# Gated linear attention into a mixture of experts: attention pieces moved together on TensorE, the state update in 64-column halves

## The chip, the cores and the metric

The kernel runs on 1 core of one Trainium2 chip. The metric is the device time of the whole launch in microseconds (us), lower is better. The span that the profile gives runs from the first to the last instruction of the program in one profiled execution.

## The reference

Two stages follow each other. For each of B = 4 batches and H = 8 heads a recurrence over S = 768 steps with head size D = 48, and then four experts on the 3072 rows that it gives:

```python
for t in range(S):
    state = alpha[:, :, t, :, None] * state + np.einsum('bhd,bhe->bhde', k[:, :, t], v[:, :, t])
    y[:, :, t] = np.einsum('bhd,bhde->bhe', q[:, :, t], state)
...
x = y.transpose(0, 2, 1, 3).reshape(B * S, H * D)        # 3072 x 384
p = domain_probs / (domain_probs.sum(-1, keepdims=True) + 1e-09)
for e in range(E):                                       # 4 experts, F = 1024
    h = np.maximum(x @ w1[e], 0.0)
    out += p[:, e:e + 1] * (h @ w2[e])
```

Everything is float32.

## The kernel before

**Units.** The sequence is cut into 6 blocks of 128 steps. One block of one batch, with its 8 heads, is a *unit*; there are 24. `attention(u)` is a Python generator that issues a unit's work in 17 *pieces*, one for each `next`; they are counted from 0 here:

- pieces 0 to 2 transpose alpha, k and q on TensorE (`turned`, L262 to L266) and copy or multiply them out of PSUM; each also issues the next unit's load on SyncE's queue;
- pieces 3 to 6 scale q and k level by level (`copy_q` on ScalarE, `next_q` on VectorE, `next_k` on both);
- piece 7 makes the *first scores*, levels 0 to 3, on TensorE (`products`, L333: 32 matmuls, each with 64 stationary columns, into PSUM tiles `sc`), and `take` (L343, VectorE) picks two of them out; piece 8 takes the other two; pieces 7 to 10 go on with `next_q`, `next_k`, `copy_q` for levels 3 to 6;
- piece 11 makes the *last scores*: 4 matmuls `far` (L388) and 16 `sc`;
- pieces 12 and 13 copy the scores into `lat` on ScalarE (L401, L405);
- piece 14, the *result*: 16 or 28 matmuls with 32 stationary columns into `yps` (L425), and a copy of it to `x_raw` on ScalarE (L441);
- piece 15 turns the scaled keys (four transposes and a copy to `AT`, L450); piece 16, the *state update*: four matmuls into `sps` with all 128 stationary columns and 96 moving columns (L454), of which only the two diagonal 64 x 48 blocks are used, and VectorE's decay and addition (L462, L463), then the load of a later unit's v. The last block of a batch has neither.

**Experts.** Units are gathered into groups of 2, 4, 4, 4, 4, 4 and 2. For each (group, expert) there is an *up* stretch of 8 chunks (`up`: matmuls `one` and `two`; from the second group on in split precision with three 128 x 128 parts, L531) and a *down* stretch (`down`: matmuls `ops`, L615 in split form, L619 in plain float32). From the third group on the hidden values are split too: for a chunk VectorE adds `one` and `two` (L544), ScalarE writes the rectified upper part `hT` (L569), VectorE the lower part (L571) and half of the difference (L581), in this order. The tiles `one`, `two` and `ops` share four PSUM buffers. The first group is in plain float32 (L523, L619), and in it the weights are split (ScalarE L223 and L225, VectorE L227 and L229).

**Order.** All is written in one program order (`tc.manual_schedule`), and each engine and queue keeps it. `deal()` gives each piece of each unit from the third on a due time on a virtual clock; `advance(cost)` moves that clock after each chunk of `up` and during `down`, and issues the pieces that have come due at that place. So the attention of the next group lies between the expert matmuls of this one. A unit's pieces are spread evenly between its `begin` and its `end`, two unit spacings apart, so two units are under way at any time:

```python
due = wanted[gis[-1]] - MARGIN
first = wanted[gi - 1] if gi > 1 else 0.0
space = (due - first) / (n if gi > 1 else (n + 1) / 2)
...
events += [(begin + (end - begin) * (j + 1) / BEATS, u, run) for j in range(BEATS)]
```

`wanted` is the virtual time at which a group's first up stretch has been left behind by the one ahead, `MARGIN` is 6. The first two units are issued by hand in a prelude and during the first expert, outside `deal()`.

Of the kernel before, what the change touches and what calls it, by code (L numbers as in the profile page):

```python
# [10 lines left out]
F32 = mybir.dt.float32  # L11
F32R = mybir.dt.float32r
# [8 lines left out]
def kernel(  # L21
# [37 lines left out]
    nc = tc.nc  # L59

    B, H, S, D = q.shape
    E, DM, F = moe_w1.shape
    P = 128
    NCB = S // P
    NP = H // 2
    HD = 64
    QUAD = 32
    TAIL = D - QUAD
    KC = DM // P
    FCH = F // P  # L70
    NT = B * P
# [10 lines left out]
    j = np.arange(P)[:, None] % HALF  # L82
    n = np.arange(QUAD)[None, :]
# [7 lines left out]
    work = ctx.enter_context(tc.tile_pool(name="work", bufs=2))  # L91
    hid = ctx.enter_context(tc.tile_pool(name="hid", bufs=2))
    ps = ctx.enter_context(tc.tile_pool(name="ps", bufs=2, space=bass.MemoryType.PSUM))
# [10 lines left out]
    lat = const.tile([P, H, P], F32, name="lat")  # L104
# [7 lines left out]
    half = B // 2  # L112
    groups = [order[:half]] + [order[i:i + B] for i in range(half, len(order), B)]
    LAST = len(groups) - 1
# [3 lines left out]
    place = {u: (gi, i) for gi, g in enumerate(groups) for i, u in enumerate(g)}  # L118
# [12 lines left out]
    def raw(u, nm):  # L131
        return values[u % 2] if nm == "v" else apart[nm] if u == 1 else early[nm]

    xTs = {}
    xraws = {}
# [7 lines left out]
    shared = {}  # L143
    accs = {}

    BEATS = 17
    MARGIN = 6.0
    waiting = deque()
    clock = 0.0
# [109 lines left out]
    def halves(t, m):  # L259
        return t.rearrange("p a (b two r) -> p a b two r", two=2, r=m)  # L260

    def turned(src):  # L262
        tp = ps.tile([P, NP, P], F32, name="tp", tag="w")
        for p in range(NP):
            nc.tensor.transpose(tp[:, p, :], src(p), ident)  # L265
        return tp  # L266

    def attention(u):
        cb, b = units[u]
        ra, rk, rq, rv = (raw(u, nm) for nm in ("a", "k", "q", "v"))  # L270
# [3 lines left out]
        AT = work.tile([P, NP, P], F32, name="AT")  # L274
        QT = work.tile([P, NP, P], F32, name="QT")
# [4 lines left out]
        KT = keys()  # L280
# [29 lines left out]
        def next_q(li):  # L310
            m = LEVELS[li]
            qv = halves(QT, m)[:, :, :, 1, :]
            dv = halved(decs[li])
            nc.vector.tensor_mul(qv, qv, spread(dv[:, :, :, 0], m))  # L314
            dec = work.tile([P, NP, P // (2 * m)], F32, name=f"dec{li}", bufs=1)
            nc.vector.tensor_mul(dec, dv[:, :, :, 0], dv[:, :, :, 1])
            decs.append(dec)

# [33 lines left out]
        for li in range(3):  # L352
            copy_q(li)
            next_q(li)
            next_k(li)
            yield
# [6 lines left out]
        for li in range(4):  # L363
            products(li, banks[li // 2][:, li % 2])
        next_q(3)
        next_k(3)
        take(0, banks[0][:, 0])
        take(1, banks[0][:, 1])
        yield
        copy_q(4)  # L370
        next_q(4)
        next_k(4)
        take(2, banks[1][:, 0])
# [12 lines left out]
        for r in range(NP // 2):  # L386
            for s in range(2):
                nc.tensor.matmul(far[HALF * s:HALF * (s + 1), r],  # L388
                                 lhsT=KTs[6][:, 2 * r + s, :HALF], rhs=qbs[6][:, 2 * r + s],
                                 start=True, stop=True)  # L390
# [8 lines left out]
        for s in range(2):  # L399
            rows = slice(HALF * s, HALF * (s + 1))  # L400
            nc.scalar.copy(out=parts[:HALF, :, s, :, HALF:], in_=far[rows])  # L401
        yield
        for s in range(2):
            rows = slice(HALF * s, HALF * (s + 1))
            nc.scalar.copy(out=lat[rows, :, rows], in_=near[rows])  # L405
        KT = KTs[-1]
        yield

        st = sts[b]
        flat_st = st.rearrange("p a i d -> p a (i d)")  # L410
        flat_v = rv.rearrange("p (a i) d -> p a (i d)", i=2)
        yps = ps.tile([P, KC, P], F32, name="yps", tag="w")
        for c in range(KC):


            if c < 2:
                now = [[(2 * c + j // 2, j % 2, (0, HD + TAIL)[j % 2], 2 * QUAD * (j % 2))
                        for j in range(4)]]
                turns = ([(True, now[0])] if cb > 0 else []) + [(False, now[0])]
            else:  # L420
                turns = [(True, [(p, 0, 0, QUAD) for p in range(NP)])] if cb > 0 else []
                turns += [(False, [(p, i, QUAD + TAIL * i, 0) for p in range(NP)]) for i in range(2)]
            for n, (past, turn) in enumerate(turns):
                for j, (p, i, in_v, in_st) in enumerate(turn):
                    nc.tensor.matmul(  # L425
                        yps[QUAD * j:QUAD * (j + 1), c, :],
                        lhsT=flat_st[:, p, in_st:in_st + QUAD] if past
                        else flat_v[:, p, in_v:in_v + QUAD],
                        rhs=QT[:, p, :] if past else lat[:, 2 * p + i, :],
                        start=(n == 0), stop=(n == len(turns) - 1))  # L430
        gi, slot = place[cb, b]
        if slot == 0:
            if gi == 0:
                xTs[gi] = work.tile([P, 3, KC, NT], F32R, name="xT", bufs=1)
                xraws[gi] = xTs[gi][:, 2].bitcast(F32)
            elif gi < LAST:
                xraws[gi] = work.tile([P, KC, NT], F32, name="x_raw", bufs=1)
            else:
                xraws[gi] = []
        if gi < LAST:  # L440
            nc.scalar.copy(out=xraws[gi][:, :, slot * P:(slot + 1) * P], in_=yps)  # L441
        else:

            xraws[gi].append(AT)
            nc.scalar.copy(out=AT[:, :KC, :], in_=yps)
        yield

        if cb < NCB - 1:
            KB = AT
            nc.scalar.copy(out=KB, in_=turned(lambda p: KT[:, p, :]))  # L450
            yield
            sps = ps.tile([P, NP, 2, D], F32, name="sps", tag="w")
            for p in range(NP):
                nc.tensor.matmul(sps[:, p], lhsT=KB[:, p, :], rhs=rv[:, 2 * p:2 * p + 2, :D],  # L454
                                 start=True, stop=True)
            for i in range(2):
                rows = slice(HD * i, HD * (i + 1))
                old, add = st[rows, :, i, :], sps[rows, :, i, :]
                if cb == 0:
                    nc.vector.tensor_copy(out=old, in_=add)  # L460
                else:
                    nc.vector.tensor_mul(old, old, decs[-1][rows].broadcast_to([HD, NP, D]))  # L462
                    nc.vector.tensor_add(old, old, add)  # L463
# [197 lines left out]
    def cost(layer, gi, e):  # L661
        n = len(groups[gi]) / 4
        if layer == 0:
            return 2.1 * n if split1(gi, e) else 2.6 * n
        return 4.1 if split2(gi, e) else 5.4

    def deal():

        wanted = [0.0]
        ends = [0.0, 0.0]
        events = []
        t = 0.0
        for (gi, e), after in zip(tasks, tasks[1:]):
            part = 1 - 1 / len(groups[0]) if gi == e == 0 else 1
            t += cost(0, gi, e) * FCH * part
            if after[1] == 0:
                wanted.append(t)
            t += cost(1, gi, e) * len(groups[gi]) * part  # L680

        for gis in [*([gi] for gi in range(1, LAST - 1)), [LAST - 1, LAST]]:
            gi, due = gis[0], wanted[gis[-1]] - MARGIN
            n = sum(len(groups[i]) for i in gis)
            first = wanted[gi - 1] if gi > 1 else 0.0
            space = (due - first) / (n if gi > 1 else (n + 1) / 2)
            if gi == 1:
                space /= 2
            for k in range(n):
                u = sum(map(len, groups[:gi])) + k  # L690
                end = due - (n - 1 - k) * space
                begin = max(end - 2 * space, ends[-2])
                ends.append(end)
                run = attention(u)
                events += [(begin + (end - begin) * (j + 1) / BEATS, u, run) for j in range(BEATS)]
        return sorted(events, key=lambda x: x[:2])

    def advance(spent):
# [5 lines left out]
    with tc.manual_schedule():  # L704
# [23 lines left out]
        def fill(n):  # L728
            for _ in range(n):
                nc.tensor.matmul(idle, lhsT=zeros, rhs=zeros, start=True, stop=True)  # L730

        runs = [attention(u) for u in range(len(groups[0]))]
        fill(8)
        for u, n in ((0, 3), (0, 6), (0, 4), (0, 5), (0, 5), (0, 4), (0, 3), (1, 0), (0, 0), (0, 2),
# [14 lines left out]
        clock = 0.0  # L749
        waiting.extend((1.0 + k, 1, runs[1]) for k in range(2))  # L750
        waiting.extend(deal())

        for (gi, e), after in zip(tasks, [*tasks[1:], (None, None)]):
# [5 lines left out]
            turns = [range(k, k + each) for k in range(rest, len(groups[gi]), each)]  # L759
# [39 lines left out]
```

## Time and profile before

| what | value |
|---|---|
| median of 8 runs | 1079.28 us (1078.24 to 1080.2) |
| profiled execution: its own time | 1080.72 us |
| profiled execution: span | 1078.9 us |
| TensorE busy (PE) | 1054.2 us, 98% of the span |
| VectorE busy (DVE) | 774.3 us, 72% |
| ScalarE busy (ACT) | 566.5 us, 53% |
| `sps` matmuls (L454) | 160 records, 21.0 us, mean 274 ns |
| `sc` matmuls (L333) | 2304 records, 76.7 us, mean 223 ns |
| `yps` matmuls (L425) | 768 and 480 records, 34.4 and 24.9 us |

A float32 matmul of the program leaves two records in the trace; one in float32r leaves one. Matmuls overlap, so the mean of one is longer than the distance between two starts. In the time order each row is a merged run of equal instructions: its start, its length, the engine, the line, the count, and in brackets the idle time before it and what ended that.

### The profile page before, as it was taken

Reading aid. Unit: us, or ns where it says so; the run is one execution under the profiler, and the core shown is the slowest. Engines: PE = TensorE matmul, PEld = TensorE weight load, DVE = VectorE, ACT = ScalarE, POOL = GpSimd, SP = SyncE. Lnnn points to the kernel's source line nnn. Section 1 sums busy time; section 2 is a strip of 40 time slices with the busy share of each in tenths; the row PEclk is TensorE's granted clock in tenths of the full one; section 3 lists DMA queues with packets and bytes.
Section 4 is the critical chain, followed back from the end, with each engine's and each line's share of the span. In section 5 each row is a group of like instructions: output and inputs, shape, how many; then the busy total and the mean of one; then the engine's idle time right before and its main releaser. Section 6 shows DMA issues by size and latency. Waiting matters only on the chain.

```text
span 1078.9 us, 21595 instructions
## 1 busy us (share of the span) xinstructions
PE 1054.2 (98%) x8460; PEld 899.2 (83%) x8460; DVE 774.3 (72%) x1711; ACT 566.5 (53%) x1202; POOL 32.7 (3%) x71
## 2 busy tenths in 40 slices
PE   8889899999999999999999999999999999999998
PEld 7767677676777798898898998888989889898988
DVE  5488678656557878778877787986887866656565
ACT  5687766664747455536446445555564543323232
POOL 2000000000000100000000000000000000000000
PEclk9999999999999999999999999999999999999999
DMA  8597679896686968659668568596594543544440
GB/s 123 155 329 218 228 234 374 303 321 240 223 300 213 400 203 312 259 146 343 214 211 331 197 220 325 163 318 231 158 359 148 241 191 140 211 174 178 184 182 31
DMA packets 158838, 251.67 MB, mean 233 GB/s; under 512 B 120112, under 2 KB 135344, under 8 KB 136208
## 3 DMA queue, kind: packets, MB, share of 16 engines
q1 hardware_dynamic: 149600, 208.82, 56.2%
q0 software_dynamic: 5760, 41.29, 9.7%
q8 instruction: 67, 1.10, 0.4%
q10 hardware_dynamic: 3376, 0.17, 0.3%
q14 instruction: 35, 0.29, 0.1%
HBM read 207.79 MB, written 42.47 MB: 232 GB/s over the span
## 4 chain that ended last, share of the span: by engine, by line
PE 81%; DVE 9%; ACT 7%; issue 2%; DMA 1%; SPq 0%; ACTq 0%; DVEq 0%
PE ops L615 26%; PE one L531 21%; PE two L531 10%; PE ops L619 9%; PE sc L333 5%; PE yps L425 4%; PE tp L265 3%; ACT qb L307 2%; PE one L523 2%; PE sps L454 1%; DVE near L343 1%; DVE hT L571 1%; PE far L388 1%; DVE t L544 1%; ACT hT L569 1%
## 5 line engine op out<-in xcount | busy, mean ns | idle before, releaser
L615 PE MATMUL ops<-w,hT 128*128 128x384 f32 x1728 | 318.9, 340 | 2.8 <-DVE acc L649 2.8
L615 PEld LDWEIGHTS ops<-w,hT 128*128 128x128 f32 x1728 | 299.4, 188 | 8.2 <-DVE acc L649 4.1
L531 PE MATMUL one<-xT,w 128*128 128x512 f32 x960 | 253.5, 399 | 0.7 <-DVE xT L247 0.5
L531 PEld LDWEIGHTS one<-xT,w 128*128 128x128 f32 x960 | 175.9, 188 | 41.5 <-issue 2.4
L542 ACT ACTIVATE t<-one 128x512 f32<-128x512 f32 (+1 forms) x192 | 106.3, 554 | 164.1 <-PE one L531 144.3
L307 ACT COPY qb<-QT 64x256 f32<-64x256 f32 x336 | 136.5, 406 | 72.1 <-DVE QT L288 35.7
L569 ACT ACTIVATE hT<-t 128x512 fp32r<-128x512 f32 (+1 forms) x160 | 94.3, 589 | 111.3 <-DVE t L544 109.9
L571 DVE SCALAR_TENSOR_TENSOR hT<-t,hT 128x512 fp32r<-128x512 f32 (+1 forms) x160 | 101.9, 637 | 60.4 <-ACT hT L569 58.6
L531 PE MATMUL two<-xT,w 128*128 128x512 f32 x480 | 136.3, 392 | 0.0
L619 PE MATMUL ops<-hT 128*128 128x384 f32 x384 | 135.0, 495 | 0.0
L544 DVE TENSOR_TENSOR t<-t,two 128x512 f32<-128x512 f32 (+1 forms) x160 | 100.7, 629 | 39.6 <-ACT t L542 21.1
L581 DVE SCALAR_TENSOR_TENSOR hT<-hT 128x256 fp32r<-128x256 f32 x288 | 112.0, 421 | 4.4
L531 PEld LDWEIGHTS two<-xT,w 128*128 128x128 f32 x480 | 90.2, 188 | 19.8
L619 PEld LDWEIGHTS ops<-hT 128*128 128x128 f32 x384 | 70.0, 192 | 40.5 <-issue 1.6
L343 DVE COPY_PREDICATED near<-masks,sc 128x256 f32<-128x256 uint8 x144 | 76.9, 534 | 18.3 <-PE sc L333 15.2
L314 DVE TENSOR_TENSOR QT<-QT,dec 128x256 f32<-128x256 f32 x144 | 60.6, 421 | 33.8 <-ACT qb L307 33.4
L333 PEld LDWEIGHTS sc<-qb,KT 128*64 128x64 f32 x2304 | 72.5, 138 | 8.9 <-issue 6.8
L333 PE MATMUL sc<-qb,KT 128*64 128x64 f32 x2304 | 76.7, 223 | 0.2 <-ACT qb L307 0.2
L649 DVE SCALAR_TENSOR_TENSOR acc<-ops,p_all,acc 128x384 f32<-128x384 f32 x82 | 49.3, 611 | 29.4 <-PE ops L615 14.4
L326 DVE TENSOR_TENSOR KT<-KT,dec 128x256 f32<-128x256 f32 x144 | 60.1, 417 | 2.3 <-PE tp L265 2.3
L325 ACT COPY KT<-KT 128x256 f32<-128x256 f32 x144 | 59.7, 415 | 3.1
L549 DVE TENSOR_TENSOR hT<-t,two 128x512 f32<-128x512 f32 x32 | 22.0, 687 | 35.2 <-ACT t L542 25.0
(88 smaller groups left out, 972.3 us busy)
## 6 DMA issues: line engine op xcount, KB each, us to landing
w<-kept SPq DMA_DIRECT2D x144, 1152.0 KB
kept<-w POOLq DMA_DIRECT2D x32, 1152.0 KB, 7.7
hT<-in_moe_w_dram SPq DMA_DIRECT2D x32, 384.0 KB
w<-in_moe_w_dram SPq DMA_DIRECT2D x48, 128.0 KB
ra<-in_alpha_dram SPq DMA_DIRECT2D x23, 192.0 KB
rk<-in_k_dram SPq DMA_DIRECT2D x23, 192.0 KB
rq<-in_q_dram SPq DMA_DIRECT2D x23, 192.0 KB
out_dram<-acc POOLq DMA_DIRECT2D x18, 192.0 KB, 6.7
```

The source lines that it names most:

```text
L307: nc.scalar.copy(out=qb[rows, :, i, :].rearrange("p a (b r) -> p a b r", r=m), in_=qv[rows])
L314: nc.vector.tensor_mul(qv, qv, spread(dv[:, :, :, 0], m))
L333: nc.tensor.matmul(out[HALF * s:HALF * (s + 1), 2 * p:2 * p + 2, :], lhsT=KTs[li][:, p, HALF * s:HALF * (s + 1)], rhs=qbs[li][:, p, :, QUA ...
L343: nc.vector.copy_predicated(near.rearrange("p a (b two r) -> p a b two r", two=2, r=m)[:, :, :, 1, :], mk.unsqueeze(1).broadcast_to([P, H, ...
L531: nc.tensor.matmul(out, lhsT=w[:, part, kc], rhs=x_part(gi, part, kc), start=(part == terms[0] and kc == 0), stop=(part == terms[-1] and k ...
L542: nc.scalar.activation(out=t, in_=one, func=ACT.Copy, scale=FINE)
L544: nc.vector.tensor_add(t, t, two)
L569: nc.scalar.activation(out=top, in_=x, func=ACT.Relu, scale=TRIM)
L571: nc.vector.scalar_tensor_tensor(out=low, in0=x, scalar=0.0, in1=top.bitcast(F32), op0=ALU.max, op1=ALU.subtract)
L581: nc.vector.scalar_tensor_tensor(out=dif, in0=top.bitcast(F32), scalar=1 / 4096.0, in1=low.bitcast(F32), op0=ALU.mult, op1=ALU.subtract)
L615: nc.tensor.matmul(sums[i][part // 2], lhsT=h[:, part], rhs=w, start=(fc == 0 and part != 1), stop=(fc == FCH - 1 and part != 0))
L619: nc.tensor.matmul(sums[i][0], lhsT=h[:, 2].bitcast(F32), rhs=w, start=(fc == 0), stop=(fc == FCH - 1))
```

## The change

Four things change; what is computed stays.

- The pieces' places in a unit's life are no longer even: piece 7 is due at 0.36 of it, 11 at 0.5, 15 at 0.86, 16 at 1.0, the others in between in proportion. With lives two spacings long, piece 15 of a unit falls on piece 7 of the next, and 16 on 11; `TOGETHER` sets them to the same time where they are less than a sixth of a spacing apart.
- From the third unit on, the keys are turned in piece 14 and the result comes in piece 15.
- The state update takes eight matmuls of 64 stationary and 48 moving columns, which give only the used blocks, side by side in the two halves of PSUM's partitions.
- A group's first unit begins `MARGIN` earlier, so all spacings are equal. `dec6` has two buffers, since it now lives across the next unit's piece 10.

On TensorE's order, 17 of the 20 state updates now stand directly ahead of `far` and the last scores of the next unit, and 20 of the 24 results directly ahead of the first scores of the next.

```diff
-    BEATS = 17
+    BEATS = [*(0.045 * (j + 1) for j in range(8)), 0.395, 0.43, 0.465, 0.5, 0.58, 0.66, 0.76, 0.86, 1.0]
+    TOGETHER = ((15, 7), (16, 11))
...
-            dec = work.tile([P, NP, P // (2 * m)], F32, name=f"dec{li}", bufs=1)
+            dec = work.tile([P, NP, P // (2 * m)], F32, name=f"dec{li}", bufs=1 + (li == 6))
...
+        def result():
+            yps = ps.tile([P, KC, P], F32, name="yps", tag="w")
...
+        def turn_keys():
+            if cb < NCB - 1:
+                nc.scalar.copy(out=AT, in_=turned(lambda p: KT[:, p, :]))
+
+
+        for step in (turn_keys, result) if u >= half else (result, turn_keys):
+            step()
+            yield
 
         if cb < NCB - 1:
             KB = AT
-            nc.scalar.copy(out=KB, in_=turned(lambda p: KT[:, p, :]))
-            yield
-            sps = ps.tile([P, NP, 2, D], F32, name="sps", tag="w")
+            sps = ps.tile([P, NP, D], F32, name="sps", tag="w")
             for p in range(NP):
-                nc.tensor.matmul(sps[:, p], lhsT=KB[:, p, :], rhs=rv[:, 2 * p:2 * p + 2, :D],
-                                 start=True, stop=True)
+                for i in range(2):
+                    rows = slice(HD * i, HD * (i + 1))
+                    nc.tensor.matmul(sps[rows, p, :], lhsT=KB[:, p, rows], rhs=rv[:, 2 * p + i, :D],
+                                     start=True, stop=True)
             for i in range(2):
                 rows = slice(HD * i, HD * (i + 1))
-                old, add = st[rows, :, i, :], sps[rows, :, i, :]
+                old, add = st[rows, :, i, :], sps[rows]
...
-            first = wanted[gi - 1] if gi > 1 else 0.0
+            first = wanted[gi - 1] - MARGIN if gi > 1 else 0.0
...
-                events += [(begin + (end - begin) * (j + 1) / BEATS, u, run) for j in range(BEATS)]
+                due_at = {-1: begin, **{j: begin + (end - begin) * BEATS[j] for j in (7, 11, 16)}}
+                for ahead, j in TOGETHER:
+                    if times and abs(times[-1][ahead] - due_at[j]) < space / 6:
+                        due_at[j] = times[-1][ahead]
+
+                beats = [0.0, *BEATS]
+                marks = sorted(due_at)
+                times.append([])
+                for lo, hi in zip(marks, marks[1:]):
+                    times[-1] += [due_at[hi] if j == hi else
+                                  due_at[lo] + (due_at[hi] - due_at[lo]) * (beats[j + 1] - beats[lo + 1])
+                                  / (beats[hi + 1] - beats[lo + 1]) for j in range(lo + 1, hi + 1)]
+                events += [(time, u, run) for time in times[-1]]
```

More of the change, by code (lines that the diff above doesn't have):

```diff
@@ L411, in attention @@
         flat_v = rv.rearrange("p (a i) d -> p a (i d)", i=2)
[L412 to L419, printed above, removed]
-            else:
[L421 to L445, printed above, removed]
@@ L446, in attention @@
-        yield
+        def result():
+            yps = ps.tile([P, KC, P], F32, name="yps", tag="w")
+            for c in range(KC):
+                if c < 2:
+                    now = [[(2 * c + j // 2, j % 2, (0, HD + TAIL)[j % 2], 2 * QUAD * (j % 2))
+                            for j in range(4)]]
+                    turns = ([(True, now[0])] if cb > 0 else []) + [(False, now[0])]
+                else:
+                    turns = [(True, [(p, 0, 0, QUAD) for p in range(NP)])] if cb > 0 else []
+                    turns += [(False, [(p, i, QUAD + TAIL * i, 0) for p in range(NP)]) for i in range(2)]
+                for n, (past, turn) in enumerate(turns):
+                    for j, (p, i, in_v, in_st) in enumerate(turn):
+                        nc.tensor.matmul(
+                            yps[QUAD * j:QUAD * (j + 1), c, :],
+                            lhsT=flat_st[:, p, in_st:in_st + QUAD] if past
+                            else flat_v[:, p, in_v:in_v + QUAD],
+                            rhs=QT[:, p, :] if past else lat[:, 2 * p + i, :],
+                            start=(n == 0), stop=(n == len(turns) - 1))
+            gi, slot = place[cb, b]
+            if slot == 0:
+                if gi == 0:
+                    xTs[gi] = work.tile([P, 3, KC, NT], F32R, name="xT", bufs=1)
+                    xraws[gi] = xTs[gi][:, 2].bitcast(F32)
+                elif gi < LAST:
+                    xraws[gi] = work.tile([P, KC, NT], F32, name="x_raw", bufs=1)
+                else:
+                    xraws[gi] = []
+            if gi < LAST:
+                nc.scalar.copy(out=xraws[gi][:, :, slot * P:(slot + 1) * P], in_=yps)
+            else:
+                xraws[gi].append(AT)
+                nc.scalar.copy(out=AT[:, :KC, :], in_=yps)
@@ L448, in attention @@
+        def turn_keys():
[4 more added lines that the diff above has]
+            yield
         if cb < NCB - 1:
             KB = AT
-            nc.scalar.copy(out=KB, in_=turned(lambda p: KT[:, p, :]))
-            yield
-            sps = ps.tile([P, NP, 2, D], F32, name="sps", tag="w")
+            sps = ps.tile([P, NP, D], F32, name="sps", tag="w")
@@ L673, in deal @@
         events = []
+        times = []
         t = 0.0
```

## The prediction

> **What bounds the kernel now.** I read the page first, then what waited for what, the groups by shape, and the time order of one up stretch on TensorE and on VectorE.
>
> ```profile
> span 1078.9 us, 21595 instructions
> ...
> PE 81%; DVE 9%; ACT 7%; issue 2%; DMA 1%; SPq 0%; ACTq 0%; DVEq 0%
> ```
>
> TensorE is busy for 98% of the span and makes 81% of the chain that ended last: what leaves TensorE's queue leaves the time, if nothing else becomes late. Its waits, longest first:
>
> ```profile
> PE yps L425 <- ACT lat L405: 8.5, 6, 3.5
> PE far L388 <- ACT qb L307: 4.6, 4, 1.6
> PE ops L615 <- DVE acc L649: 2.8, 4, 1.2
> ```
>
> The result waits 8.5 us for the score copies, nearly all of it while the first group's experts run. The stretches (columns: length, then PE, PEld, DVE, ACT, POOL busy with counts, granted clock, DMA) show that one, and an up stretch of the split part:
>
> ```profile
> 45.00:171.00 126.00, 116.90 (x1123) 89.73 (x1116) 92.04 (x197) 91.66 (x202) 9.18 (x17) 0.97 0.77 253
> ...
> 526.46:548.62 22.16, 22.16 (x206) 17.91 (x205) 18.35 (x39) 14.56 (x30) 1.07 (x2) 1.00 0.98 391
> ```
>
> In the first the granted clock is 0.97, so 0.03 x 126 = 3.8 us went on a slower clock, which followed the longest waits. In the second VectorE works 18.35 of 22.16 us. TensorE's time order in it (start, length, count):
>
> ```profile
> 541.36 1.64 PE L531 MATMUL one<-xT,w 128*128 128x512 f32 x6
> 542.83 0.85 PE L531 MATMUL two<-xT,w 128*128 128x512 f32 x3
> 543.62 2.08 PE L333 MATMUL sc<-qb,KT 128*64 128x64 f32 x64
> 545.63 1.65 PE L531 MATMUL one<-xT,w 128*128 128x512 f32 x6
> 547.12 0.85 PE L531 MATMUL two<-xT,w 128*128 128x512 f32 x3
> 547.81 1.02 PE L454 MATMUL sps<-rv,AT 128*128 128x96 f32 x8
> 548.62 2.55 PE L615 MATMUL ops<-w,hT 128*128 128x384 f32 x13
> ```
>
> Undisturbed, three `two` take 0.69 from start to next start (547.12 to 547.81), six `one` 1.37. Ahead of `sc` the three take 0.79: going into 64-column form costs 0.10. Behind it the six take 1.49: 0.12. In between lie 2.01 us; the start times in the trace put pairs of records (two column halves) 58 ns apart, so 32 pairs are 1.86 and the first pair's delay and the way out are 0.15. **One visit to 64-column form costs 0.37 us** beside its work. The same reading of the result's 28 matmuls (starts 534.31, 535.09, 536.76, with 14 groups of four at 110 ns) gives 0.09 + 0.13 + 0.12 = **0.34** for 32 columns. The old state update needs no visit: 0.81 from 547.81 to 548.62, and the next thirteen `ops` are 0.08 late: 0.89 us, which is 8 records at the 111 ns at which 128-column records follow each other.
>
> **Part A, the state update in halves.** New work: 8 matmuls, 16 records, 8 pairs. The trace has no 64x48 records; the nearest row is `sc` (64 columns, 64 wide) at 58 ns a pair: 0.46 us. Bounds: 48/64 of it, 0.35; and no overlap of halves, 0.93. I take 0.46, since pairs of exactly this column form overlap in `sc`. For 17 updates the visit is paid by `far` behind them: 17 x (0.89 - 0.46) = 7.3 us. Three stand alone and pay 0.37: 3 x (0.89 - 0.83) = 0.2. **Together -7.5.** The Trainium skill ("TensorEngine Tiling (Array Packing)", Instruction Overhead) speaks against cutting the moving side: it says that a matmul with one moving column takes as long as one with about 60, so 48 would cost what 60 costs. By that rule the 0.35 is out of reach and the term stays as it is.
>
> **Part B, result and first scores in one go.** Twenty times two visits (0.37 + 0.34) become one visit and one change from 32- to 64-column form, which the trace doesn't show. Bounds: free (like staying in one form, `far` to `sc`), which saves 0.35 each, 6.9 in all; or a full visit, which saves nothing. I take about 0.15, the part of a visit that is paid inside it, because the late start of the wide matmuls behind (0.12) and the way in from them (0.10) fall away: 0.2 saved each, **-4.1**. The same page (Tiling Modes, Key Properties) says that changing the tiling mode drains TensorE. By it the free bound is excluded for this switch, which agrees with taking a price above zero.
>
> **Part C, the first group's stretch (45 to 171 us).** The result moves from directly behind the `lat` copies (a seventeenth of a life) to 0.2 of a life behind them, with the turned keys between. Of the 8.5 us about 8.0 belong to units under `deal()`; they go, with about half of the slow clock behind them, 2 us. What is late next is `far` on `copy_q`: pieces 7 to 11 close up from 0.235 to 0.14 of a life. The shortest chain from the scores' start is: first scores' half 1.3, two takes 1.3 (546.27 to 547.57), level 4's q, dec, k and two takes 1.6, level 5's q 0.33, two `copy_q` on ScalarE 0.8: 5.4 us, or 3.3 behind the scores' end. TensorE's new order leaves there, with L619 at 0.645 us a matmul and L523 at 0.43: unit 2, 3.9 us; unit 3, 1.3 + 0.46; unit 4, 5.0; unit 5, 3.7. So unit 3 waits 1.6 us at least, and each waits up to 1.9 us more where a split weight piece (L227 and L229, 0.95 each) lies in between: 1.6 to 7, I take 3.5, plus 1 for other late things as the same copies are pushed on. **-8.0 - 2 + 4.5 = -5.5**; bounds -12 (all the clock back, no new wait but 1.6 less) and +3 (the waits come back as `far`).
>
> **Part D, the crowded up stretches.** Before, the first scores stand after the fifth or sixth of the eight chunks and `far` in the down stretch. After, in some nine up stretches of split experts, pieces 7 to 11 and 16 all lie in one up stretch: scores after chunk 0, `far` after chunk 5. VectorE's cadence there:
>
> ```profile
> 537.55 0.68 DVE L544 TENSOR_TENSOR t<-t,two 128x512 f32<-128x512 f32 x1
> 538.93 0.69 DVE L571 SCALAR_TENSOR_TENSOR hT<-t,hT 128x512 fp32r<-128x512 f32 x1 [0.70 <-ACT hT L569]
> ...
> 540.00 0.68 DVE L544 TENSOR_TENSOR t<-t,two 128x512 f32<-128x512 f32 x1
> ```
>
> A chunk turns round in 2.45 us through VectorE and ScalarE (add 0.60, wait for `hT` 0.78, low 0.73, difference 0.34) against 2.06 on TensorE, and attention work on VectorE hides only in the 0.78. Counting from add 0: result and scores hold TensorE for 3.8 us, so add 1 is at 5.9. Add 1 to 2 holds piece 8: 0.6 + 0.2 (rest of `copy_q`) + 1.57 + 1.07 = 3.4. Piece 9 fits nearly: 2.5. Then 2.45 and 2.45. Add 5 to 6 holds the state update's 1.6 and piece 11's 1.14: 4.4. Then 2.45. Add 7 is at 23.5. TensorE ends the same chunk's `two` at 5.8 + 4 x 2.06 + (0.46 + 1.8) + 2 x 2.06 + 0.44 = 20.9. So VectorE is 2.6 us behind, where before it was 0.9 (548.66 against 547.8). `far` itself isn't late: its last `copy_q` ends at about 14.5, and TensorE comes to it at 14.0 + 0.1 + 0.46. But the down stretch's seventh matmul (22.3) needs the buffer that ScalarE reads at 22.4 to 23.0, behind chunk 6's `hT`: 0.8; the second down half needs accumulations that are then 0.3 late. 1.1 x 9 = 10, less the 3 to 4 of such waits that are there now (2.8 on `acc`, and others below 0.3): **+6**. Bounds: -3 (the buffers are slack enough) and +20 (2.6 us late in each of nine).
>
> Transpositions and other TensorE work only change places. The next loads go with pieces 0 to 2 and 16 on SyncE's queue as before, and no load is waited for more than 0.7 us now. The second `dec6` buffer costs nothing.
>
> **Sum.** -7.5 - 4.1 - 5.5 + 6 = -11.1. The profiled execution has its own time of 1080.72 (span 1078.9): 1069.6. The median of the runs is 1.4 below it: 1068.2.
>
> **The rivals.**
>
> *VectorE becomes the bound in the up stretches* (slower). Place: the same nine stretches. For: 18.35 of 22.16 us busy there already, and a cadence of 2.45 against 2.06. Against: the four buffers let TensorE be a chunk ahead, and the down stretch has 14.80 us of VectorE work in 21.38. If each of the nine loses the whole 2.6 and the 1.1, that is 33 - 3.5: 1079.3 - 17.1 + 29.5 = 1092. It decides from 2.3 us per stretch, where it eats the other parts' 17.
>
> *The halves don't overlap and the change of form is a full visit* (the change doesn't do what it says). Then A is 17 x 0.04 + 3 x 0.41 = +1.9 and B is 0: 1079.3 + 1.9 - 5.5 + 6 = 1081.7, or 1079 with half of D. Against: `sc` pairs start 6 to 8 ns apart.
>
> *No new wait counts and the change of form is free.* A -7.5, B -6.9, C -12, D 0: 1053. Against: the cadence above.
>
> **How the numbers follow.** Forecast 0.70, VectorE as the bound 0.12, no overlap 0.06, all gains at their best 0.12. The range 1056 to 1081 takes in B's bounds and most of C's and D's, and leaves out the tails of the two outer cases. A measurement can tell 0.2% (2.2 us) from no change: faster below 1077.1, slower above 1081.4. The forecast's upper tail puts 0.03 into "same", and the second rival is halved between "same" and slower: faster 0.79, same 0.06, slower 0.15.
>
> **What would show it.** Right: the `sps` matmuls 0.46 us a block with `far` directly behind; `yps` waiting under 1 us on `lat`; the clock in 45 to 171 us nearer 1.00; PE busy about 10 us less; `far` on `qb` up by some 3 us; waits of `ops` on VectorE or ScalarE of about 1 us once per task in the middle of the kernel. Wrong: `sps` blocks near 0.9; a wide matmul or `two` waiting for L544 inside up stretches for more than 2 us each; waits for `x_raw` or a DMA that aren't there now.

## The result and the profile after

The changed kernel is slower: 1087.04 us (median of 11 runs, 1085.65 to 1089.17) against 1079.72 us of 30 runs of the kernel before, a ratio of 1.0067 with a 95% interval of 1.006 to 1.0075. The forecast was 1068.2, the range 1056 to 1081. The profiled execution took 1087.35 us with a span of 1085.6; before it was 1080.72 and 1078.9.

The page of the changed kernel, its span and the chain that ended last:

```profile
span 1085.6 us, 21981 instructions
...
PE 74%; DVE 13%; ACT 6%; DMA 3%; issue 2%; SPq 1%; DVEq 0%; ACTq 0%
```

TensorE's share of the chain fell from 81% to 74%. Its busy time fell too, from 1054.2 to 1049.4 us; what grew is its waiting. The view of what TensorE waited for (us, times, longest):

```profile
PE far L391 <- ACT qb L310: 16.7, 9, 3.4
PE sc L336 <- ACT qb L310: 5.3, 7, 1.5
PE ops L628 <- DVE acc L662: 3.3, 5, 1.6
PE one L544 <- DVE xT L250: 1.8, 1, 1.8
```

The result's 8.5 us of waits on `lat` are down to 0.5. In their place `far` waits 16.7 us instead of 4.6, and the first scores, which had 0.2, wait 5.3. All waits together went from 20.7 to 32.1 us. By place: of `far`'s waits 11.2 us lie between 45 and 183 us, and so do all 5.3 us of the first scores. The same stretch by windows (length, busy time of the five engines, granted clock, then DMA):

```profile
45.00:183.00 138.00, 120.67 (x1176) 92.22 (x1176) 95.71 (x211) 96.12 (x212) 9.19 (x17) 0.95 0.75 238
...
63.00:66.40 3.40, 3.40 (x15) 2.06 (x12) 3.33 (x11) 2.91 (x7) 0.00 (x0) 0.50 1.06 424
93.70:97.10 3.40, 3.40 (x37) 2.62 (x33) 2.13 (x7) 0.00 (x0) 0.00 (x0) 0.51 0.50 146
```

The granted clock there is 0.95 (0.97 before). The records show four stretches of 3.4 us at half clock, two of them in the rows above; before there were two. Each costs up to 1.7 us.

The change itself does what it says (in the changed kernel L467 makes the state update, L391 `far`, L336 the scores, L430 the result, L544 `one` and `two`). TensorE's time order around a joined state update and around a joined result:

```profile
510.12 0.86 PE L544 MATMUL two<-xT,w 128*128 128x512 f32 x3
510.91 0.67 PE L467 MATMUL sps<-rv,AT 128*64 128x48 f32 x16
511.42 0.62 PE L391 MATMUL far<-qb,KT 128*64 128x128 f32 x8
511.87 1.10 PE L336 MATMUL sc<-qb,KT 128*64 128x64 f32 x32
512.90 1.66 PE L544 MATMUL one<-xT,w 128*128 128x512 f32 x6
```

```profile
497.65 0.62 PE L430 MATMUL yps<-lat,rv 128*32 128x128 f32 x16
498.20 2.08 PE L336 MATMUL sc<-qb,KT 128*64 128x64 f32 x64
500.21 1.67 PE L544 MATMUL one<-xT,w 128*128 128x512 f32 x6
```

The joined block of update, `far` and scores delays the wide matmuls by 2.19 us where `far` and scores alone do by 1.72: the update costs 0.47. Result and first scores together cost 3.89, apart 1.87 and 2.22: 0.20 saved (from the start times in the trace, blocks behind 370 us without a wait).

### The profile page after: what moved, and what is told of

It reads as the page before. It is cut to its first block, busy times and chain, and to the rows that moved or that the text cites. A ratio compares the mean times of both kernels' runs of the same rounds, so it can differ in the third digit from the quotient of the medians.

```text
span 1085.6 us, 21981 instructions
## 1 busy us (share of the span) xinstructions
PE 1049.4 (97%) x8620; PEld 892.5 (82%) x8620; DVE 771.7 (71%) x1711; ACT 568.8 (52%) x1202; POOL 32.8 (3%) x71
## 4 chain that ended last, share of the span: by engine, by line
PE 74%; DVE 13%; ACT 6%; DMA 3%; issue 2%; SPq 1%; DVEq 0%; ACTq 0%
PE ops L628 23%; PE one L544 20%; PE two L544 10%; PE ops L632 9%; PE sc L336 5%; PE yps L430 3%; PE tp L268 2%; ACT qb L310 2%; DVE t L557 2%; DVE near L346 2%; DVE hT L584 2%; DMA w<-in_moe_w_dram 1%; PE one L536 1%; DVE hT L594 1%; DVE QT L317 1%
## 5 line engine op out<-in xcount | busy, mean ns | idle before, releaser
L628 PE MATMUL ops<-w,hT 128*128 128x384 f32 x1728 | 314.8, 339 | 3.4 <-DVE acc L662 3.3
L544 PE MATMUL one<-xT,w 128*128 128x512 f32 x960 | 256.1, 401 | 2.0 <-DVE xT L250 1.8
L544 PEld LDWEIGHTS one<-xT,w 128*128 128x128 f32 x960 | 176.7, 188 | 44.5 <-DVE xT L250 2.7
L544 PE MATMUL two<-xT,w 128*128 128x512 f32 x480 | 137.8, 395 | 0.0
L632 PE MATMUL ops<-hT 128*128 128x384 f32 x384 | 135.4, 500 | 0.0
L557 DVE TENSOR_TENSOR t<-t,two 128x512 f32<-128x512 f32 (+1 forms) x160 | 100.6, 629 | 43.4 <-PE two L544 25.2
L544 PEld LDWEIGHTS two<-xT,w 128*128 128x128 f32 x480 | 90.1, 188 | 22.0
L632 PEld LDWEIGHTS ops<-hT 128*128 128x128 f32 x384 | 71.6, 195 | 42.9 <-issue 2.8
L336 PE MATMUL sc<-qb,KT 128*64 128x64 f32 x2304 | 80.4, 227 | 5.3 <-ACT qb L310 5.3
L336 PEld LDWEIGHTS sc<-qb,KT 128*64 128x64 f32 x2304 | 75.2, 141 | 11.4 <-ACT qb L310 6.6
L317 DVE TENSOR_TENSOR QT<-QT,dec 128x256 f32<-128x256 f32 x144 | 60.7, 421 | 23.8 <-ACT qb L310 23.7
L329 DVE TENSOR_TENSOR KT<-KT,dec 128x256 f32<-128x256 f32 x144 | 60.1, 417 | 0.0
L536 PE MATMUL one<-xT,w 128*128 128x256 f32 (+1 forms) x240 | 45.9, 340 | 0.6 <-ACT xT L446 0.6
```

Of the source, the lines that this page charges most:

```text
L336: nc.tensor.matmul(out[HALF * s:HALF * (s + 1), 2 * p:2 * p + 2, :], lhsT=KTs[li][:, p, HALF * s:HALF * (s + 1)], rhs=qbs[li][:, p, :, QUA ...
L544: nc.tensor.matmul(out, lhsT=w[:, part, kc], rhs=x_part(gi, part, kc), start=(part == terms[0] and kc == 0), stop=(part == terms[-1] and k ...
L557: nc.vector.tensor_add(t, t, two)
L628: nc.tensor.matmul(sums[i][part // 2], lhsT=h[:, part], rhs=w, start=(fc == 0 and part != 1), stop=(fc == FCH - 1 and part != 0))
L632: nc.tensor.matmul(sums[i][0], lhsT=h[:, 2].bitcast(F32), rhs=w, start=(fc == 0), stop=(fc == FCH - 1))
```

## The experiments

The theory was *pace*: under the first expert group a unit has only about 23 us of real time per spacing, and pieces 3 to 11 in half a life leave ScalarE and VectorE too little time for the chain of `copy_q`, `next_q` and `next_k`. The rivals were *crowded up stretches* (the forecast's own fear) and *equal spacing* (each group's first unit begins earlier). Ratios are to the kernel before, with the 95% interval; "the stretch" is the first group's, from 45 us on. Each kernel was made from the changed one, unless another is named.

**The old pace under the first group.**

```diff
+                pace = [(j + 1) / 17 for j in range(17)] if gi == 1 else BEATS
...
-                for ahead, j in TOGETHER:
+                for ahead, j in TOGETHER if gi > 1 else ():
```

> The changed kernel, but the four units that are dealt out under the first expert group keep the old even pace (seventeenths of a life) and nothing there is set together. Theory 'pace': the changed kernel loses its time between 45 and 183 us, where far and the first scores wait 11.2 and 5.3 us for copy_q because pieces 3 to 11 have half a life there, about 23 us of real time; with the old pace those waits fall to about 1.6 us as before, the granted clock there goes back from 0.95 to 0.97 or more, some of the 7.3 us of waits on lat come back (not all: the turned keys now lie between), and the four results and updates lose their neighbours (4 x 0.2 and 4 x 0.35 us). 1087 - 13 + 4 = about 1075, between 1071 and 1078, and so faster than the kernel before. Rival 'crowded up stretches': the loss is made where pieces 7 to 11 and 16 share an up stretch, which stays as it is: 1085 or more. Rival 'equal spacing': the earlier start of each group's first unit makes VectorE late at group boundaries: also stays, 1085.

Measured: 1078.62 us, 0.9992 (0.9982 to 1.0001). From 1.0067 that is 8 us less, so *pace* has a large share; but 1075 and a gain were expected, and the result is no better than the kernel before. Of the 11.2 us of `far` in the first stretch 2.5 are left, of the first scores' 5.3 only 0.2; 4.1 us on `lat` come back. What is new against the kernel before stands at the end of it and behind it, on TensorE:

```profile
PE tp L268 <- DMA rk<-in_k_dram: 2.7, 1, 2.7
PE one L544 <- DVE xT L250: 1.8, 1, 1.8
```

**The new pace alone.** This is the changed kernel with all else put back, the keys turned first under the first group and the second `dec6` buffer excepted.

```diff
...
+                pace = BEATS if gi == 1 else [(j + 1) / 17 for j in range(17)]
...
```

> The kernel before with one part of the change: the four units dealt out under the first expert group take the new places (piece 7 at 0.36, 11 at 0.5, 15 at 0.86 of a life, keys turned first), all else stays, the wide state update and the even pace of the later groups too. Theory 'pace': this alone costs what the first stretch lost, 11 to 13 us, 1090 to 1093. If the loss needs the halves, the joined visits of later groups or the equal spacing: 1079 to 1082.

Measured: 1089.46 us, 1.0087 (1.0073 to 1.0101), 9.4 us more, just under the 11 to 13 that were expected. Neither halves nor joined visits of later groups nor equal spacing are needed for it. The waits between 45 and 177 us have the names of the changed kernel's, those of the first scores the size too:

```profile
PE far L391 <- ACT qb L310: 8.5, 4, 3.1
PE sc L336 <- ACT qb L310: 5.3, 7, 1.5
```

Not all of the 9.4 us is the pace. The profiled execution is the fastest of the four (1087.62, the others 1089.2 to 1090.2 at a lower granted clock). Against the kernel before, TensorE waits 4.7 us longer in it, with as many stretches at half clock, and is busy for 2.2 us longer; the section on the prediction comes back to that.

**Only `far` later.** Under the first group, pieces 8 to 13 at 0.42, 0.48, 0.54, 0.60, 0.66 and 0.72 of a life.

> The changed kernel; in the first group's stretch only pieces 8 to 13 are later (piece 11 at 0.6 of a life instead of 0.5), pieces 0 to 7 and the result keep the new places. Theory 'pace': of the waits there the 11.2 us of far go to 2 or less, those of the first scores (5.3 us, pieces 3 to 7 too close) stay; two of the four stretches at half clock go. 1087 - 9 - 3 + 1 = about 1077, 1074 to 1081. If the backlog of the whole chain counts and not where far stands: 1084 to 1087.

Measured: 1078.74 us, 0.9992 (0.9982 to 1.0001), inside what *pace* expected. `far` waits 1.8 us in the stretch, the first scores still 5.9. So the two waits are separate: `far` comes from the close places of 7 to 11, the first scores from those of 3 to 7.

**The second group's first unit begun no earlier**, with the old pace under the first group.

```diff
-            first = wanted[gi - 1] - MARGIN if gi > 1 else 0.0
+            first = wanted[gi - 1] - (MARGIN if gi > 2 else 0.0) if gi > 1 else 0.0
```

> The changed kernel with the old even pace for the units under the first expert group, and the second expert group's first unit begun no earlier than before (the later groups' first units still begin earlier). It asks where the rest of the expected gain is held: with the even pace alone the run still had 1.8 us of wait for VectorE's split of x as the second expert group begins, a stretch at half clock behind it, and 1.1 us of far. If the earlier first unit crowds VectorE there: that wait falls to about 0.7 as in the kernel before and the half clock behind it goes: 1078.6 - 1.1 - 1.7 = about 1076. If the wait comes from the last unit's own late pieces: 1078 to 1079.

Measured: 1071.87 us, 0.9928 (0.9915 to 0.9941). This one condition is worth 0.64%, 6.9 us, more than twice the 2.8 expected. *Equal spacing* was thus the second half of the loss. The wait for VectorE's split of x falls from 1.8 to 0.4 us, `far`'s waits of 0.8 us ahead of it and 1.1 behind it are gone, and the records have one stretch at half clock instead of three. One of the two that are gone, at 82 us in the kernel with the old pace, is not the edit's work: it follows a wait of 2.3 us at 80 us that both kernels have, and TensorE's order is the same in both up to 130 us. So of the 6.9 us up to 1.7 may be chance of where the wait falls (last section). How the earlier unit gets in the way shows on VectorE in the changed kernel:

```profile
183.84 0.69 DVE L251 SCALAR_TENSOR_TENSOR xT<-xT 128x512 fp32r<-128x512 f32 x1
184.45 0.42 DVE L317 TENSOR_TENSOR QT<-QT,AT 128x256 f32<-128x256 f32 x1
184.79 0.42 DVE L319 TENSOR_TENSOR dec<-AT 128x256 f32<-128x256 f32 x1
185.12 0.42 DVE L329 TENSOR_TENSOR KT<-KT,AT 128x256 f32<-128x256 f32 x1
185.46 0.68 DVE L250 TENSOR_TENSOR xT<-x_raw,xT 128x512 fp32r<-128x512 f32 x1
```

The next unit's first level (L317 to L329, 1.0 us) stands between two parts of the split of x, while TensorE has nothing but these parts to wait for.

**The weight loads behind k and q**, on top of that. The last kernel had one long wait left, 3.9 us for k, which was issued behind twelve weight loads on SyncE's queue; the order on the queue was the same before, but TensorE now comes for k earlier (at 131.7 us, where it was 142.1).

```diff
-        if gi == 0 and ends and e + 1 < E and fc == (0 if e == 0 else FCH // 2):
+        if gi == 0 and ends and e + 1 < E and fc == (0 if e == 0 else FCH // 2 + 2):
```

> As the kernel with the even pace under the first expert group and the second group's first unit not begun earlier, but the next expert's weight loads of the first layer are issued two chunks later under the first expert group, so that the next unit's k and q go ahead of these twelve loads on SyncE's queue. In that kernel TensorE waited 3.9 us for k, which was issued behind them, and ran at half clock for 3.4 us after it. If only the order on the queue made k late: 3.9 + 1.7 us less, 1066 to 1068. If the loads as such are late (the queue waits for buffers): the wait goes over to a weight piece, 1071 to 1074.

Measured: 1067.25 us, 0.9889 (0.9873 to 0.9906), as the first line expected. This version beats both kernels. Its page and what TensorE still waits for:

```profile
PE 1043.4 (98%) x8620; PEld 888.4 (83%) x8620; DVE 771.5 (72%) x1711; ACT 566.7 (53%) x1202; POOL 32.8 (3%) x71
```

```profile
PE far L391 <- ACT qb L310: 5.8, 5, 1.5
PE yps L430 <- ACT lat L408: 4.4, 3, 2.3
PE ops L628 <- DVE acc L662: 3.4, 5, 1.7
```

No wait for a DMA is in the list, and no stretch at half clock until the end of the program.

**The halves alone**, in the kernel before (the eight narrow matmuls and `sps[rows]`, nothing else).

> The kernel before with only the state update changed to eight matmuls of 64 stationary and 48 moving columns; order and pace are the old ones. If a visit to 64-column form costs 0.37 us beside its work, a lone update takes 0.47 + 0.36 = 0.83 against 0.89: 20 x 0.06 = 1.2 us less, 1078.5. If the halves alone carried the gain of 0.42 each, 8 us less: 1071. If a lone visit costs more than a wide update saves: 1081.

Measured: 1078.92 us, 0.9991 (0.9978 to 1.0004); the 1.2 us that were expected lie inside the interval. By the trace's start times a lone update delays the wide matmuls by 0.80 us, against 0.89 in wide form. Most of the halves' saving needs the neighbour.

**The wide update at the new places.**

```diff
-                    nc.tensor.matmul(sps[rows, p, :], lhsT=KB[:, p, rows], rhs=rv[:, 2 * p + i, :D],
...
+                nc.tensor.matmul(sps[:, p], lhsT=KB[:, p, :], rhs=rv[:, 2 * p:2 * p + 2, :D],
...
```

> The changed kernel with the old wide state update (four matmuls of 128 stationary and 96 moving columns) at its new places. If the halves next to far save 0.42 us for each of 17 and little for three: 7 us more, 1094. If the waits in the first stretch swallow part of it (four of the updates stand there): 5 us more, 1092. If the halves saved nothing: 1087.

Measured: 1088.68 us, 1.0091 (1.0068 to 1.0115), 2.6 us more than the changed kernel, with intervals that overlap; 5 to 7 were expected. The four runs lie apart by clock: 1086.2 and 1086.5 us at 0.998, 1090.8 and 1091.1 at 0.994. The changed kernel's runs at 0.994 took 1086.9 to 1087.4, so at equal clock the wide update costs about 4 us more. The blocks differ by the 0.40 us forecast (from the wide matmul before to the one behind, 2.71 against 2.31), 17 of them. But in the profiled executions, both with four stretches at half clock, the sum of TensorE's waits is 29.3 instead of 32.1: 2.8 us of the gain are waited away again, 1.5 of them on VectorE's accumulation.

**The result apart from the first scores.** Pieces 14 and 15 at 0.72 and 0.78 of a life, and (15, 7) taken out of `TOGETHER`.

> The changed kernel with the result and the turned keys earlier (0.78 and 0.72 of a life instead of 0.86 and 0.76), so that the result stands alone, not ahead of the next unit's first scores. If one visit less is worth 0.20 us each for 18 to 20: 3.6 to 4 us more, 1091. If the change of form from 32 to 64 columns costs as much as a visit: no change, 1087. In the first stretch the waits may move by some us either way, so the blocks between undisturbed wide matmuls are to be read too: 1.87 + 2.22 us apart against 3.89 together.

Measured: 1089.66 us, 1.0107 (1.0082 to 1.0133), 4.3 us more than the changed kernel. That this is near the expected 3.6 to 4 is luck: two runs took 1087.0 and 1087.3 us at a clock of 0.995 and 0.994, as long as the changed kernel, and two 1092.1 and 1092.2 at 0.992 and 0.991. In the profiled one (1087.26) TensorE is busy 2.7 us longer and waits 2.9 us less, so the total doesn't show the saving. The blocks do: 1.86 and 2.22 us apart, 3.89 together.

**What stretches the chain.** Two kernels left out parts of the weight splitting. The first replaced all of it:

> The changed kernel with the splitting of the first layer's weights left out (ScalarE's two copies and VectorE's two operations a piece, 16 pieces, all under the first expert group; GpSimd fills the pieces with zeros instead, and they are written to memory as before). It asks what makes the chain of copies slow there. If the weight splitting's turns in ScalarE's and VectorE's queues (0.84 x 2 and 0.95 x 2 us a piece) stretch the chain: waits of far and first scores in 45 to 183 us fall from 16.5 to 5 or less, about 1073. If the chain is too long by itself for half a life of 23 us: they stay above 10, about 1083.

Measured: 1104.31 us, 1.0227 (1.0208 to 1.0246). It can't be read as meant: TensorE waited 33.1 us for weights from memory up to 68 us, a wait that no other run has. Between 45 and 183 us `far` waited 4.1 us and the first scores 0.3. The second kept ScalarE's copies and their pace and left out VectorE's two operations:

```diff
+        if l == 0:
+            nc.gpsimd.memset(low.bitcast(F32), 0.0)
...
```

> The changed kernel, where VectorE's two operations of the first layer's weight splitting are left out (16 pieces, 1.9 us each; GpSimd fills one part with zeros instead; ScalarE's two copies and the write to memory stay and keep their pace). If VectorE's turns for the weights between the pieces' operations stretch the chain to far and first scores under the first expert group: the 16.5 us of these waits between 45 and 183 us fall by half or more, 1076 to 1080. If ScalarE's copies or the chain itself set the pace: they fall by less than a quarter, 1084 to 1087.

Measured: 1078.25 us, 0.9984 (0.9975 to 0.9993). Between 45 and 183 us:

```profile
PE far L394 <- ACT qb L313: 5.4, 5, 2.2
PE sc L339 <- ACT qb L313: 4.5, 7, 1.5
```

16.5 us of waits became 9.9, four tenths less, which is between the two expectations; the time, with one stretch at half clock instead of four, is where the first put it. So VectorE's turns for the weights make about 6.6 us of the 16.5, mostly of `far`'s; a new wait of 2.7 us for a load of q takes part of that back. The rest is put down to the chain itself and ScalarE's queue, which no run separates.

**Two tunings that gave nothing.** With the pace under the first group at 0.055 of a life a piece up to piece 11, copies at 0.72 and 0.78, keys at 0.88, result at 0.96:

> The changed kernel with another pace in the first group's stretch: pieces 0 to 11 evenly up to 0.66 of a life, the copies at 0.72 and 0.78, keys turned at 0.88, result at 0.96, nothing joined there. Theory 'pace': the waits on lat that were left with the even pace (4.1 us there) fall below 2 as the result moves away from the copies, those of far stay near 2.5: 1075 to 1077, faster than the kernel before by 0.2 to 0.4%. If the late result only pushes its wait on to other things: 1079.

Measured: 1080.61 us, 1.0012 (1.0003 to 1.002). The waits on `lat` are gone, but the first scores wait 8.2 us: the wait moved, as its rival said. And with the result 0.03 of a life later, joined to the next first scores:

> As the one with the old even pace under the first expert group and the second group's first unit not begun earlier, but the result of those four units comes 0.03 of a life later, together with the next one's first scores. Two or three visits less (0.2 us each), and the waits of the result on lat, 4.1 us there with the even pace, have 0.7 virtual us more to pass: 2 us or more less, 1074. If what delays the copies is ScalarE's queue as a whole, the wait goes from the result to the first scores and nothing is gained: 1076 to 1079.

Measured: 1072.49 us, 0.9932 (0.9918 to 0.9945), no better than without it. The result waits 2.8 us instead of 4.1, the first scores 1.0 instead of 0.4, k 4.5 instead of 3.9.

## Why the prediction was wrong

**Part A held.** A joined update takes 0.47 us (0.46 forecast); 17 x 0.40 + 3 x 0.09 = 7.1 us less, 7.5 were forecast. The two halves of a pair start 6 to 7 ns apart and the next pair 58 ns later, as with 64 columns.

**Part B held,** as far as single blocks show it: 0.20 us a visit, 20 times, 4 us. The change from 32- to 64-column form is neither free nor a full visit.

**Part C failed, and it carries the result.** Forecast: -5.5 with a bound of +3. Measured in that stretch: TensorE's waits 17.4 against 9.3 us, and two more stretches at half clock, worth at most 3.4: 8.1 + 3.4 = +11.5. Three terms of it were wrong:
- `far` on `copy_q` was put at 3.5 us, within 1.6 to 7; it was 11.2. The sum took the shortest chain from the first scores' start and at most one weight piece beside it. In the trace the two units' operations and the weights share two queues in order. This is unit 3 in the changed kernel, all engines in order of time:

```profile
84.75 0.43 DVE L317 TENSOR_TENSOR QT<-QT,dec 128x256 f32<-128x256 f32 x1 [0.35 <-ACT qb L310]
85.34 0.83 ACT L228 ACTIVATE w<-w 128x768 fp32r<-128x768 f32 x1
86.07 0.81 ACT L310 COPY qb<-QT 64x256 f32<-64x256 f32 x2
86.93 0.69 PE L336 MATMUL sc<-qb,KT 128*64 128x64 f32 x16 [1.47 <-ACT qb L310]
...
90.66 0.82 ACT L310 COPY qb<-QT 64x256 f32<-64x256 f32 x2 [0.84 <-DVE QT L317]
92.20 0.82 ACT L310 COPY qb<-QT 64x256 f32<-64x256 f32 x2 [0.29 <-DVE dec L319]
93.07 0.66 PE L391 MATMUL far<-qb,KT 128*64 128x128 f32 x8 [3.37 <-ACT qb L310]
```

  ScalarE copies a weight part (L228) and only then the fourth level's q, for which the last quarter of the first scores waits 1.47 us. From there to `far` three more turns between ScalarE and VectorE follow, and TensorE, with four L632 records and the update to do, waits 3.37 us.
- The first scores had no term of their own, only a share in the 1 us for "other late things". Pieces 3 to 7 also lie closer, 0.045 instead of 0.059 of a life each: 5.3 us.
- The half clock was booked as a gain, -2. New waits of 2.0 to 3.4 us brought it back twice as often. The upper bound of +3 was no bound, since it let the waits come back only as far as they had been.

**An edit costed at nothing was not free.** That each group's first unit begins `MARGIN` earlier was listed in the change and given no term. For the second group it puts a unit's first pieces on VectorE between the parts of the split of x: with the old pace it was worth 6.9 us, two stretches at half clock among them, of which one may be chance. The forecast let the work "only change places" without asking what stands at a group's end.

**Part D was too pessimistic.** +6 was forecast for the crowded up stretches; from 372 us on TensorE waits 4.9 us against 3.9 before. VectorE does lag as forecast: in the up stretch shown above its last addition (L557) starts at 520.07 us, 2.3 us behind the end of the `two` that it adds, where 2.6 were forecast. But the lag is absorbed, as the first rival's counter-argument had it: `ops` waits once per group or so, 0.2 to 1.6 us, not 1.1 us in each of nine stretches. The rival of VectorE as the bound there is refuted: slower was right, for another reason and at another place.

The terms as measured: -7.1 - 4 + 11.5 + 1.0, and 2.4 for the waits between 183 and 372 us (2.9 against 0.5), make +3.8; the spans differ by 6.7. The remaining 2.9 us lie in TensorE's busy time. A likely place for them shows, but no cause. In the kernel with the new pace alone, TensorE's order from 156 us on is that of the kernel before, matmul for matmul. Still `one` and `two` are busy for longer there, first the kernel before, then this one:

```profile
L531 PE MATMUL one<-xT,w 128*128 128x512 f32 x960 | 253.5, 399 | 0.7 <-DVE xT L247 0.5
L531 PE MATMUL two<-xT,w 128*128 128x512 f32 x480 | 136.3, 392 | 0.0
```

```profile
L542 PE MATMUL one<-xT,w 128*128 128x512 f32 x960 | 256.9, 402 | 1.0 <-DVE xT L250 1.0
L542 PE MATMUL two<-xT,w 128*128 128x512 f32 x480 | 137.8, 395 | 0.0
```

That is 4.9 us more; `ops` is busy 1.7 us less, so 3.2 us remain. By the start times behind 200 us, undisturbed `two` follow each other at 229 ns on average in the kernel before and the one with the halves alone, and at 232 to 233 in all twelve others. These twelve have the second `dec6` buffer, of which the forecast says that it "costs nothing". No run changes the buffer alone, so whether it is the cause stays open.

With the three stumbling blocks removed, the kernel comes out at 1067.25, within 1 us of the forecast. That is a coincidence: it gives up the joined visits under the first group, and has one edit that the change does not have.

## What to carry to other kernels

A pace that is given in proportion to a life is a different pace in each stage: look up the shortest life, and price there the whole chain between two engines with everything else that their queues hold, not the shortest path through it. When pieces are drawn together to save TensorE's changes of form, the saving in a block is small (0.2 to 0.4 us each here), and what feeds the pieces decides; check each group boundary, where TensorE has no other work to go on with. A wait of two microseconds can cost nearly four when the clock goes down behind it.

## What the runs showed of the hardware

The half-clock stretches follow a fixed grid of 3.4 us. Laying that grid over TensorE's busy time in these runs, a window that it idled for 2.0 us or more was always followed by one at half clock; one idle for less than 1.55 us never was, and between these either happened. (The kernel with all of the weight splitting left out is excepted: it stayed at half clock for 44 us, through windows that were idle for less.) So the place of a wait in the grid counts too: the same wait of 2.3 us at 80 us lies in one window in the kernel with the old pace under the first group, which ran at half clock behind it; with the second group's unit begun later as well, a border splits it into 1.3 and 1.0 us, and the clock stayed. The Trainium skill ("TensorE: Matmul & The Clock Gate", Part 1) says that the clock goes down after at least one idle window of about 3.4 us. The runs agree with the window's length, but not with the need for a whole idle one: 2.0 us of waits, in pieces, were enough.

A change from 32- to 64-column form costs about 0.15 us beside the work, and a visit to either form 0.33 to 0.36. The same skill ("TensorEngine Tiling (Array Packing)", Key Properties) speaks of a drain at each change of mode; the blocks together and apart give it this size.
